# One neighbour step for both base tiles, float32r matmuls behind 512-wide ones, and a single ring of PSUM banks in a fused attention and MLP kernel

## The chip, the cores and the metric

The kernel runs on one core of one Trainium2 chip. The time is device microseconds (us) of one execution, and the metric is the median over runs. A run more than 1.5% above the fastest of the same kernel is called slow here and is left out of ratios. TensorE is called PE, VectorE DVE, ScalarE ACT, as in the profile.

## The reference

```python
def _attn_ref(x, inducing):            # x [4, 12480, 128], inducing [32, 128]
    ...
    def mab(q, kv):
        s = scale * (q @ kv.transpose(0, 2, 1))
        s = s - s.max(-1, keepdims=True)
        a = np.exp(s)
        a /= a.sum(-1, keepdims=True) + 1e-09
        return a @ kv
    h = mab(I, x)                      # 32 rows per batch
    return mab(x, h)

def _moe_ref(x, w_in, w_out):          # w_in [128, 2048], w_out [2048, 128]
    h = x @ w_in
    relu6 = np.clip(h + 3.0, 0.0, 6.0)
    return (h * relu6 / 6.0) @ w_out
```

The second attention mixes only 32 rows h of its batch. Where the hidden values stay inside the clip's range, the MLP of such a mix is a linear term in the 32 weights plus a quadratic one in the pairs of weights. So the kernel first reads a batch to find its h and makes coefficients from it; then each token needs only exponentials, and matmuls against the coefficients.

## The kernel before

A batch has 25 chunks: 24 of four tiles of 128 tokens, and a short one. Four chunks are a group; the short chunk is a group by itself. For each chunk, two matmuls `bp` and their exponentials give two **base tiles** of pair features. The column set `W[k]` holds h(m) + h(m+2+2k+4i), so base 0 has the pairs at distances 2, 6, 10, ... and base 1 those at 4, 8, 12, ... The odd distances come from a **neighbour step**: base 0 times exp(h(m+1) - h(m)) gives distances 1, 5, ..., and times exp(h(m-1) - h(m)) gives 3, 7, ...

```python
# coefficients of a batch
Wd = coef.tile([P, 2, M], BF16, name="Wd")            # two neighbour steps
nc.vector.tensor_sub(Wd[:, 0], HT2[:, 1 : M + 1], HT[:, 0])           # shortened
nc.vector.tensor_sub(Wd[:, 1], HT2[:, M - 1 : 2 * M - 1], HT[:, 0])   # shortened
...
def b_pack(b, g, k):            # one group's neighbour factors, k = 0, 1
    pp = psF.tile([P, 512], FP32, name="pp", tag="fb")
    for j in range(J):          # four tiles of 32 columns, side by side
        nc.tensor.matmul(pp[32 * j : 32 * j + 32, :w], lhsT=st["Wd"][:, k], rhs=..., tile_position=(0, 32 * j))
    t = dpk.tile([P, 512], BF16, name=f"dk{k}")
    nc.scalar.activation(t[: 32 * J, :w], pp[: 32 * J, :w], ACT.Exp, scale=scale)
def b_spread(b, c):             # each row to four partitions, by DMA
    for k in range(2):
        d = dp.tile([P, 512], BF16, name=f"d{k}")
        nc.sync.dma_start(d[:, :w], st[("dk", g, k)][...].unsqueeze(1).to_broadcast([32, 4, w]))
def b_prod(b, c):
    for k in range(2):
        d = st.pop(("d", c, k))
        nc.vector.tensor_mul(t[:, :w], T0[:, :w], d[:, :w])
...
def b_f(b, g):                  # sums of the exponentials e
    nc.tensor.matmul(sp[:, : J * p], lhsT=blk[:, :], rhs=e[:, : J * p])          # float32r
    # nf = -e * sp
def b_r(b, g):                  # 1 / sum, a whole group at once
    for j in range(J):
        nc.tensor.matmul(rp[:p, j * SL : (j + 1) * SL], lhsT=nf[:, j * p : (j + 1) * p], rhs=one4[:, :])  # float32r
    nc.vector.reciprocal(r_all[...], rp[:p, : J * SL])
def b_lin(b, c):                # linear term, float32r, 512 columns
    nc.tensor.matmul(op[:p, :], lhsT=nf[...], rhs=BD, start=True, stop=False)
def b_quad(b, c, s, op):        # quadratic term of one of four token tiles
    for k in range(4):
        nc.tensor.matmul(op[:p, s * C : (s + 1) * C], lhsT=T[k][:, s * p : (s + 1) * p], rhs=Cq[:, k, :])
```

While batch b gives out its results, batch b+1 is read (`xb`, `pt`, `xT`, `s`, `a`, `hnd`) and its coefficients are made: G (`gp`) and its hardswish `hs`, `L`, `BD`; `dpm` and its squares `sq`; their sums `cp`, then `Cq`. These pieces are "units", emitted between the parts of a chunk:

```python
for t in range(-LEAD - 3, total):           # one chunk; b_evac, b_spread, b_prod cut
    b_base(fb_, fc, 0)                      # bp for chunk t + 2
    bg(0.25)                                # units due by here
    op = b_lin(bo, co); b_quad(bo, co, 0, op)
    bg(0.5)
    b_quad(bo, co, 1, op)
    for fn in ahead.get(t, []): fn()        # b_pack | b_e | b_f | b_r, each in its own chunk of the group
    bg(0.75)
    b_quad(bo, co, 2, op)
    b_base(fb_, fc, 1)
    bg(1.0)
    b_quad(bo, co, 3, op)
```

PSUM has three banks in a pool `psF` (bp, pp, ep, sp, rp), two in `psX` (pt, s, dpm), two for the output and one (`psH`) for hnd, gp, lp and cp.

## Time and profile before

I cut the run at the starts of the linear products (`op<-BD,nf`) of chunks 0, 25, 50 and 75 and of the last chunk. What lies ahead of the first is the start-up; the tail is the last evacuation and the checks at the end.

| before | us |
|---|---|
| time, median of 4 runs (range; the 363.68 is a slow run) | 356.44 (354.2 to 363.68) |
| start-up | 54.00 |
| batches 0, 1, 2 (with background) | 82.62, 79.93, 79.28 |
| last batch (no background) | 46.28 |
| tail | 10.70 |
| span of the profiled run (a run of its own, 354.64) | 352.80 |

The last batch is the clean place to price an instruction, because nothing but chunks runs there. The background batches are where most of the time is. The profile's own lines stand in the prediction.

### The profile page before, as it was taken

To read this page: it belongs to the slowest core of one execution; us is meant where nothing else is said; L and a number is where in the kernel's file an instruction comes from. 1 tells how busy PE (TensorE), PEld (TensorE's weight loads), DVE (VectorE), ACT (ScalarE), POOL (GpSimd) and SP (SyncE) were. 2 spreads that over 40 slices of the span, in tenths; PEclk is the share of its full clock that TensorE was granted. 3 is DMA by queue.
4 is the path that set the end of the run, shared out by engine and by line. 5 is a ranking of instruction groups with operands and counts; after the bars stand their busy time and mean duration, and the time that the engine had idled before them with its cause. 6 is when DMAs were issued, how large, how long until landed. Compare 5 with 4: busy or idle time off the path is not lost. (4 is left out here: it accounts for less than half of the span.)

```text
span 352.8 us, 10094 instructions
## 1 busy us (share of the span) xinstructions
PE 321.2 (91%) x4001; PEld 238.6 (68%) x4026; DVE 245.5 (70%) x592; ACT 239.3 (68%) x440; POOL 17.6 (5%) x37
## 2 busy tenths in 40 slices
PE   0968989999969999999999999999999999999990
PEld 0855567787646676887667676887667776676670
DVE  4765777787587556877696556877696656777781
ACT  2433589877546988888556988888556885767740
POOL 3032000101100000010100000010000000000000
PEclk9999899999999999999999999999999999999996
DMA  7699744697994665778996576687673566789963
GB/s 268 226 349 361 271 92 91 163 333 242 354 357 156 157 178 190 204 256 217 342 403 237 136 206 194 180 258 239 144 208 132 140 207 199 224 254 252 256 211 130
DMA packets 38536, 79.54 MB, mean 225 GB/s; under 512 B 5168, under 2 KB 31824, under 8 KB 32208
## 3 DMA queue, kind: packets, MB, share of 16 engines
q1 hardware_dynamic: 32560, 51.15, 47.8%
q0 software_dynamic: 5920, 27.66, 25.2%
q8 instruction: 33, 0.54, 0.6%
q14 instruction: 23, 0.19, 0.2%
HBM read 27.67 MB, written 25.56 MB: 151 GB/s over the span
## 5 line engine op out<-in xcount | busy, mean ns | idle before, releaser
L594 PE MATMUL op<-Cq,T 128*128 128x128 bf16 (+1 forms) x1600 | 147.5, 220 | 0.5
L558 ACT ACTIVATE T<-bp 128x512 bf16<-128x512 f32 (+1 forms) x200 | 112.4, 593 | 42.6 <-PE bp L552 30.6
L594 PEld LDWEIGHTS <-T 128*128 128x128 bf16 (+1 forms) x1600 | 98.0, 98 | 42.4 <-issue 26.4
L610 DVE TENSOR_TENSOR os<-op,r_all 128x512 f32<-128x512 f32 (+1 forms) x100 | 68.7, 687 | 47.2 <-PE op L594 46.4
L569 DVE TENSOR_TENSOR T<-T,d 128x512 bf16<-128x512 bf16 (+1 forms) x200 | 74.1, 409 | 7.2 <-DMA d<-dk 6.9
L552 PE MATMUL bp<-xT,W 128*128 128x512 bf16 (+1 forms) x186 | 69.4, 374 | 0.8 <-DVE d_all L328 0.8
L206 ACT CAST xb<-xr 128x1024 bf16<-128x1024 f32 (+1 forms) x49 | 46.8, 963 | 9.6 <-DMA xr<-in_x_dram 9.6
L578 PE MATMUL op<-BD,nf 128*128 128x512 f32 (+1 forms) x100 | 52.3, 523 | 0.0
L216 DVE COPY xT<-pt 128x1024 bf16<-128x1024 bf16 (+1 forms) x56 | 34.4, 618 | 11.8 <-PE pt L215 11.5
L237 PE MATMUL hnd<-xr,a 128*32 128x128 f32 (+1 forms) x400 | 38.0, 237 | 3.2 <-ACT a L229 3.2
L427 ACT ACTIVATE sq<-dpm 128x512 bf16<-128x512 f32 x60 | 35.3, 603 | 7.0 <-PE dpm L416 5.2
L529 ACT ACTIVATE dk<-pp 128x512 bf16<-128x512 f32 (+1 forms) x56 | 28.2, 554 | 13.3 <-PE pp L522 12.7
L215 PE MATMUL pt<-ident_b,xb 128*128 128x128 bf16 (+1 forms) x400 | 32.7, 225 | 4.7 <-DVE xb L206 4.1
L237 PEld LDWEIGHTS hnd<-xr,a 128*32 128x32 f32 (+1 forms) x400 | 27.5, 111 | 9.7 <-ACT a L229 5.2
L215 PEld LDWEIGHTS <-xb 128*128 128x128 bf16 (+1 forms) x400 | 25.7, 101 | 10.5 <-DVE xb L206 4.2
L111 POOL DMA_DIRECT2D xr<-in_x_dram x28 | 15.1, 539 | 219.2 <-ACT xb L206 127.9
L436 PE MATMUL cp<-w6n,sq 128*128 128x128 bf16 x256 | 24.3, 219 | 1.6 <-DVE BD L409 0.9
L229 ACT ACTIVATE a<-s 128x512 fp32r<-128x512 f32 (+1 forms) x28 | 15.5, 553 | 15.0 <-PE s L223 15.0
L436 PEld LDWEIGHTS <-sq 128*128 128x128 bf16 x256 | 18.6, 98 | 9.2 <-DVE BD L409 1.4
L416 PE MATMUL dpm<-dH,w_in_b 128*128 128x512 bf16 x54 | 20.8, 389 | 2.7 <-DVE dH L350 2.6
L487 DVE CUSTOM_DVE_ANT_0 nf<-e,sp 128x512 fp32r<-128x512 f32 (+1 forms) x28 | 17.2, 613 | 4.7 <-PE sp L485 4.2
L552 PEld LDWEIGHTS <-W 128*128 128x128 bf16 x200 | 19.5, 98 | 0.6
(98 smaller groups left out, 270.3 us busy)
## 6 DMA issues: line engine op xcount, KB each, us to landing
xr<-in_x_dram POOLq DMA_DIRECT2D x24, 1024.0 KB, 7.5
d<-dk SPq DMA_DIRECT2D x192, 128.0 KB, 3.9
out_dram<-os SPq DMA_DIRECT2D x24, 1024.0 KB, 4.1
w_in_r<-in_moe_w_in_dram POOLq DMA_DIRECT2D x1, 1024.0 KB, 5.8
w_out_r<-in_moe_w_out_dram POOLq DMA_DIRECT2D x1, 1024.0 KB, 9.6
xr<-in_x_dram POOLq DMA_DIRECT2D x4, 96.0 KB, 5.9
d<-dk SPq DMA_DIRECT2D x8, 48.0 KB, 3.7
out_dram<-os SPq DMA_DIRECT2D x4, 96.0 KB, 3.2
```

The lines of the kernel that those rows point to most:

```text
L206: eng(xb[:p, lo:hi, :], xs[(b, g)][:p, lo:hi, :].bitcast(FP32))
L215: nc.tensor.transpose(pt[:, (i - lo) * p : (i - lo + 1) * p], xb[:p, i, :], ident_b[:p, :p])
L216: nc.vector.tensor_copy(st["xT"][:, t0 + lo * p : t0 + hi * p], pt[:, : (hi - lo) * p])
L237: nc.tensor.matmul(st["hnd"][:M, :C], lhsT=a1[:p, i * M : (i + 1) * M], rhs=xs[(b, g)][:p, i, :], start=(g == 0 and i == 0), stop=(g == NG ...
L427: nc.scalar.activation(sq[:, :], dpm[:, :], ACT.Square)
L436: nc.tensor.matmul(st["cp"][:, k * C : (k + 1) * C], lhsT=sq[:, k * P : (k + 1) * P], rhs=w6n[:, jc, :], start=(jc == 0 and k == 0), stop= ...
L552: nc.tensor.matmul(bp[:, :w], lhsT=st["W"][:, k].rearrange("p m i -> p (m i)"), rhs=st["xT"][:, c0 : c0 + w],)
L558: nc.scalar.activation(t[:, :w], bp[:, :w], ACT.Exp, scale=scale)
L569: nc.vector.tensor_mul(t[:, :w], T0[:, :w], d[:, :w])
L578: nc.tensor.matmul(op[:p, :], lhsT=st[("nf", g)][:, j * p : (j + 1) * p], rhs=st["BD"][:, :], start=True, stop=False, skip_group_check=True,)
L594: nc.tensor.matmul(op[:p, s * C : (s + 1) * C], lhsT=T[k][:, s * p : (s + 1) * p], rhs=st["Cq"][:, k, :], start=False, stop=(s == SL - 1 a ...
L610: nc.vector.tensor_mul(ot[:p, j * SL : (j + 1) * SL, :], op[:p, :].rearrange("p (s c) -> p s c", c=C), r_all[:p, b, c, :].unsqueeze(2).to_ ...
```

## The change

The intent: shorten PE's stream, since PE sets the time.

1. One neighbour step d = exp(h(m+1) - h(m)) for **both** base tiles. Base 0 times d has distances 1, 5, ...; base 1 times the same d pairs m+1 with m+4+4i, distances 3, 7, ... Half of pp, of its exponentials, and of the transfers go away, and one multiply of 1024 columns replaces two of 512. pp and ep are emitted together.
2. rp is taken one chunk at a time, behind a `bp`.
3. sp stands behind the other `bp`.
4. So does the linear product, in every chunk (behind sp where there is one).
5. For batches 1 to 3, the G matmuls stand singly behind the 512-wide dpm.
6. For batches 1 to 3, the coefficient sums cp follow after all 16 squares.
7. psF and psX become one ring of five banks, which cp of batches 1 to 3 also draws on.
8. Smaller things go with it: the four products of a tile are taken in the order 0, 3, 1, 2 (base tiles first), and `hs` becomes a unit of its own.

```diff
-        psF = es.enter_context(tc.tile_pool(name="psF", bufs=3, space=PSUM))
+        psF = es.enter_context(tc.tile_pool(name="psF", bufs=5, space=PSUM))
-        psX = es.enter_context(tc.tile_pool(name="psX", bufs=2, space=PSUM))
...
-            Wd = coef.tile([P, 2, M], BF16, name="Wd")
+            Wd = coef.tile([P, M], BF16, name="Wd")
...
+                us += [lambda jb=jb: (c_sq(b, jb), c_G(b, jb, jb + 1)) for jb in range(FB)]
+                us += ls[0:1] + cs[0:4] + ls[1:3] + cs[4:8] + ls[3:] + cs[8:]
...
+            nc.tensor.matmul(rp[:p, :SL], lhsT=nf[:, j * p : (j + 1) * p], rhs=one4[:, :])
+            nc.vector.reciprocal(r_all[:p, b, c, :], rp[:p, :SL])
...
+            u = tp.tile([P, 2, 512], BF16, name="TD")
+            nc.vector.tensor_mul(u[:, :, :w], t[:, :, :w], d[:, :w].unsqueeze(1).to_broadcast([P, 2, w]))
+            st[("T", c)] = [t[:, 0], u[:, 0], u[:, 1], t[:, 1]]
...
-            for k in range(4):
+            for k in (0, 3, 1, 2):
...
+                ahead.setdefault(t - LEAD - 3, []).append(lambda b=b, g=g: (b_pack(b, g), b_e(b, g)))
+                sums[t - LEAD - 1] = (b, g)
...
             if feat:
                 b_base(fb_, fc, 0)
-            bg(0.25)
+            if t in sums:
+                b_f(*sums[t])
             if t >= 0:
                 op = b_lin(bo, co)
                 b_quad(bo, co, 0, op)
-            bg(0.5)
+            bg(0.33)
...
-            bg(0.75)
+            bg(0.67)
+            if feat:
+                b_base(fb_, fc, 1)
+            if 0 <= t + 1 < total:
+                b_r(*divmod(t + 1, NCK))
             if t >= 0:
                 b_quad(bo, co, 2, op)
-            if feat:
-                b_base(fb_, fc, 1)
```

More of the change, by code (lines that the diff above doesn't have):

```diff
@@ L27 @@
 XBUF = 4
-CLAG = 6
 LEAD = 2
@@ L92 @@
         cst = es.enter_context(tc.tile_pool(name="cst", bufs=1))
-        sqp = es.enter_context(tc.tile_pool(name="sqp", bufs=8))
+        sqp = es.enter_context(tc.tile_pool(name="sqp", bufs=FB))
         coef = es.enter_context(tc.tile_pool(name="coef", bufs=2))
         PSUM = bass.MemoryType.PSUM
-        psF = es.enter_context(tc.tile_pool(name="psF", bufs=3, space=PSUM))
+        psF = es.enter_context(tc.tile_pool(name="psF", bufs=5, space=PSUM))
         psO = es.enter_context(tc.tile_pool(name="psO", bufs=2, space=PSUM))
-        psX = es.enter_context(tc.tile_pool(name="psX", bufs=2, space=PSUM))
         psH = es.enter_context(tc.tile_pool(name="psH", bufs=1, space=PSUM))
@@ L186, in side_bank @@
                     return psO.tile(shape, dtype, name=name, tag="op")
-            return psX.tile(shape, dtype, name=name, tag="pt")
+            return psF.tile(shape, dtype, name=name, tag="fb")
         S = {}
@@ L349, in c_HT, with c_G @@
             nc.vector.tensor_sub(dH[:, 0], shifted(HT, 0, 1, 0), shifted(HT, 2, 0, 4))
-            nc.vector.tensor_sub(dH[:, 1], shifted(HT, M - 1, 1, 0), shifted(HT, 2, 2, 4))
+            nc.vector.tensor_sub(dH[:, 1], shifted(HT, 1, -1, 0), shifted(HT, 4, 0, 4))
             W = coef.tile([P, 2, M, 4], BF16, name="W")
             nc.vector.tensor_add(W[:, :], shifted(HT, 0, 0, 0), shifted(HT, 2, 2, 4))
-            Wd = coef.tile([P, 2, M], BF16, name="Wd")
-            nc.vector.tensor_sub(Wd[:, 0], HT[:, :, :].rearrange("p a m -> p (a m)")[:, 1 : M + 1], HT[:, 0])
-            nc.vector.tensor_sub(Wd[:, 1], HT[:, :, :].rearrange("p a m -> p (a m)")[:, M - 1 : 2 * M - 1], HT[:, 0])
+            Wd = coef.tile([P, M], BF16, name="Wd")
+            nc.vector.tensor_sub(Wd[:, :], HT[:, :, :].rearrange("p a m -> p (a m)")[:, 1 : M + 1], HT[:, 0])
             st["W"], st["Wd"] = W, Wd
-        def c_G(b, h):
+        def c_G(b, lo, hi):
             st = S[b]
-            if h == 0:
+            if lo == 0:
                 st["gp"] = psH.tile([P, 512], FP32, name="gp", tag="hnd")
             gp = st["gp"]
-            for jb in range(8 * h, 8 * h + 8):
+            for jb in range(lo, hi):
                 nc.tensor.matmul(
@@ L369, in c_G, with c_hs @@
                 )
-            if h == 0:
-                return
+        def c_hs(b):
+            st = S[b]
+            gp = st["gp"]
             r6 = cst.tile([P, 512], FP32, name="r6")
@@ L413, in c_sq, with c_C @@
             st = S[b]
-            if jb < FB:
-                dpm = side_bank(b, [P, 512], FP32, "dpm")
-                nc.tensor.matmul(
-                    dpm[:, :],
-                    lhsT=w_in_b[:, jb * P : (jb + 1) * P],
-                    rhs=st["dH"][:, :, :, :, :].rearrange("p q k m i -> p (q k m i)"),
-                )
-                sq = sqp.tile([P, 512], BF16, name="sq")
-                if b == 0 and jb % 4 == 3:
-                    d32 = cst.tile([P, 512], FP32, name="d32")
-                    nc.vector.tensor_copy(d32[:, :], dpm[:, :])
-                    nc.vector.tensor_mul(sq[:, :], d32[:, :], dpm[:, :])
-                else:
-                    nc.scalar.activation(sq[:, :], dpm[:, :], ACT.Square)
-                st[("sq", jb)] = sq
-            jc = jb - CLAG
-            if jc < 0:
-                return
+            dpm = side_bank(b, [P, 512], FP32, "dpm")
+            nc.tensor.matmul(
+                dpm[:, :],
+                lhsT=w_in_b[:, jb * P : (jb + 1) * P],
+                rhs=st["dH"][:, :, :, :, :].rearrange("p q k m i -> p (q k m i)"),
+            )
+            sq = sqp.tile([P, 512], BF16, name="sq")
+            if b == 0 and jb % 4 == 3:
+                d32 = cst.tile([P, 512], FP32, name="d32")
+                nc.vector.tensor_copy(d32[:, :], dpm[:, :])
+                nc.vector.tensor_mul(sq[:, :], d32[:, :], dpm[:, :])
+            else:
+                nc.scalar.activation(sq[:, :], dpm[:, :], ACT.Square)
+            st[("sq", jb)] = sq
+        def c_C(b, jc):
+            st = S[b]
             if jc == 0:
-                st["cp"] = psH.tile([P, 512], FP32, name="cp", tag="hnd")
+                st["cp"] = (psH if b == 0 else psF).tile([P, 512], FP32, name="cp", tag="hnd" if b == 0 else "fb")
             sq = st.pop(("sq", jc))
@@ L454, in c_units @@
         def c_units(b):
-            sq = [lambda jb=jb: c_sq(b, jb) for jb in range(FB + CLAG)]
             gap = [lambda: None]
             us = [lambda: c_sum(b)] + gap + [lambda: c_den(b)] + gap + [lambda: c_HT(b)] + gap
-            us += sq[0:1] + [lambda: c_G(b, 0), lambda: c_G(b, 1)] + sq[1:3]
-            us += [lambda: c_L(b, 0), lambda: c_L(b, 1)] + sq[3:5] + [lambda: c_BD(b)]
-            us += sq[5:] + [lambda: c_tail(b)]
-            return us
+            cs = [lambda jc=jc: c_C(b, jc) for jc in range(FB)]
+            ls = [lambda: c_hs(b), lambda: c_L(b, 0), lambda: c_L(b, 1), lambda: c_BD(b)]
+            if b == 0:
+                sq = [lambda jb=jb: c_sq(b, jb) for jb in range(FB)]
+                us += sq[0:1] + [lambda: c_G(b, 0, 8), lambda: (c_G(b, 8, FB), c_hs(b))] + sq[1:3]
+                us += ls[1:3] + sq[3:5] + ls[3:] + sq[5:7]
+                for jb in range(7, FB):
+                    us += [cs[jb - 7], sq[jb]]
+                us += cs[FB - 7 :]
+            else:
+                us += [lambda jb=jb: (c_sq(b, jb), c_G(b, jb, jb + 1)) for jb in range(FB)]
+                us += ls[0:1] + cs[0:4] + ls[1:3] + cs[4:8] + ls[3:] + cs[8:]
+            return us + [lambda: c_tail(b)]
         def b_e(b, g):
@@ L497, in b_f, with b_r, b_pack @@
             st[("nf", g)] = nf
-        def b_r(b, g):
+        def b_r(b, c):
+            g, j = chunks[c]
             t0, p, n = groups[g]
-            st = S[b]
-            J = n // SL
-            nf = st[("nf", g)]
+            nf = S[b][("nf", g)]
             rp = psF.tile([P, 512], FP32, name="rp", tag="fb")
-            for j in range(J):
-                nc.tensor.matmul(
-                    rp[:p, j * SL : (j + 1) * SL], lhsT=nf[:, j * p : (j + 1) * p], rhs=one4[:, :]
-                )
-            c0 = first_chunk[g]
-            nc.vector.reciprocal(
-                r_all[:p, b, c0 : c0 + J, :].rearrange("p j s -> p (j s)"), rp[:p, : J * SL]
-            )
-        def b_pack(b, g, k):
+            nc.tensor.matmul(rp[:p, :SL], lhsT=nf[:, j * p : (j + 1) * p], rhs=one4[:, :])
+            nc.vector.reciprocal(r_all[:p, b, c, :], rp[:p, :SL])
+        def b_pack(b, g):
             t0, p, n = groups[g]
@@ L523, in b_pack @@
                     pp[32 * j : 32 * j + 32, :w],
-                    lhsT=st["Wd"][:, k],
+                    lhsT=st["Wd"][:, :],
                     rhs=st["xT"][:, t0 + j * w : t0 + (j + 1) * w],
@@ L527, in b_pack @@
                 )
-            t = dpk.tile([P, 512], BF16, name=f"dk{k}")
+            t = dpk.tile([P, 512], BF16, name="dk")
             nc.scalar.activation(t[: 32 * J, :w], pp[: 32 * J, :w], ACT.Exp, scale=scale)
-            st[("dk", g, k)] = t
+            st[("dk", g)] = t
         def b_spread(b, c):
@@ L536, in b_spread @@
             w = SL * groups[g][1]
-            for k in range(2):
-                d = dp.tile([P, 512], BF16, name=f"d{k}")
-                nc.sync.dma_start(
-                    d[:, :w],
-                    st[("dk", g, k)][32 * j : 32 * j + 32, :w].unsqueeze(1).to_broadcast([32, 4, w]),
-                )
-                st[("d", c, k)] = d
+            d = dp.tile([P, 512], BF16, name="d")
+            nc.sync.dma_start(
+                d[:, :w],
+                st[("dk", g)][32 * j : 32 * j + 32, :w].unsqueeze(1).to_broadcast([32, 4, w]),
+            )
+            st[("d", c)] = d
         def b_base(b, c, k):
@@ L556, in b_base @@
             )
-            t = tp.tile([P, 512], BF16, name=f"T{3 * k}")
-            nc.scalar.activation(t[:, :w], bp[:, :w], ACT.Exp, scale=scale)
-            st[("x", c, k)] = t
+            if k == 0:
+                st[("x", c)] = tp.tile([P, 2, 512], BF16, name="TF")
+            nc.scalar.activation(st[("x", c)][:, k, :w], bp[:, :w], ACT.Exp, scale=scale)
         def b_prod(b, c):
@@ L563, in b_prod @@
             w = SL * groups[chunks[c][0]][1]
-            T0, T3 = (st.pop(("x", c, k)) for k in range(2))
-            T = [T0]
-            for k in range(2):
-                d = st.pop(("d", c, k))
-                t = tp.tile([P, 512], BF16, name=f"T{1 + k}")
-                nc.vector.tensor_mul(t[:, :w], T0[:, :w], d[:, :w])
-                T.append(t)
-            st[("T", c)] = T + [T3]
+            t = st.pop(("x", c))
+            d = st.pop(("d", c))
+            u = tp.tile([P, 2, 512], BF16, name="TD")
+            nc.vector.tensor_mul(u[:, :, :w], t[:, :, :w], d[:, :w].unsqueeze(1).to_broadcast([P, 2, w]))
+            st[("T", c)] = [t[:, 0], u[:, 0], u[:, 1], t[:, 1]]
         def b_lin(b, c):
@@ L598, in b_quad @@
                     start=False,
-                    stop=(s == SL - 1 and k == 3),
+                    stop=(s == SL - 1 and k == 2),
                     skip_group_check=True,
@@ L646 @@
         total = B * NCK
-        ahead = {}
+        ahead, sums = {}, {}
         for b in range(B):
@@ L650 @@
                 t = b * NCK + first_chunk[g]
-                ahead.setdefault(t - LEAD - 3, []).append(lambda b=b, g=g: (b_pack(b, g, 0), b_pack(b, g, 1)))
-                ahead.setdefault(t - LEAD - 2, []).append(lambda b=b, g=g: b_e(b, g))
-                ahead.setdefault(t - LEAD - 1, []).append(lambda b=b, g=g: b_f(b, g))
-                ahead.setdefault(t - LEAD, []).append(lambda b=b, g=g: b_r(b, g))
+                ahead.setdefault(t - LEAD - 3, []).append(lambda b=b, g=g: (b_pack(b, g), b_e(b, g)))
+                sums[t - LEAD - 1] = (b, g)
         for b in range(1, B):
```

## The prediction

> **What bounds the kernel now.** I read the page first, then the busy time of each engine in chosen stretches, then the timeline of TensorE (PE) in the last batch. The kernel has a start-up of 54 us, then four batches of 25 chunks. While batches 0 to 2 give out their results, the next batch is read in and its coefficients are made ("background"); the last batch has none.
>
> ```profile
> PE 321.2 (91%) x4001; PEld 238.6 (68%) x4026; DVE 245.5 (70%) x592; ACT 239.3 (68%) x440; POOL 17.6 (5%) x37
> ...
> 0.00:54.00 54.00, 39.16 (x468) 29.03 (x472) 34.92 (x85) 25.69 (x43) 8.55 (x20) 0.97 0.83 256
> ...
> 136.63:216.55 79.92, 78.12 (x999) 58.70 (x1004) 57.48 (x136) 60.95 (x113) 3.73 (x7) 1.00 0.76 242
> 295.83:342.11 46.28, 46.28 (x539) 32.83 (x540) 36.00 (x90) 32.24 (x63) 0.00 (x0) 1.00 0.86 248
> ```
>
> The columns of a stretch are its length, then busy us of PE, weight load, VectorE (DVE), ScalarE (ACT), GpSimd. PE is busy for 78.1 of 79.9 us in batch 1 and for all of the last batch; DVE and ACT stand at 72 and 76% in batch 1. So PE's instruction stream sets the time after 54 us, and what shortens it shortens the run, until another engine comes up to it. What an instruction costs there is the distance between starts, not its printed length (lengths overlap). The stream in the last batch:
>
> ```profile
> 326.05 0.58 PE L578 MATMUL op<-BD,nf 128*128 128x512 f32 x1
> 326.48 0.62 PE L594 MATMUL op<-Cq,T 128*128 128x128 bf16 x8
> 327.03 0.62 PE L522 MATMUL pp<-xT,Wd 128*32 128x512 bf16 x8
> 327.58 0.40 PE L594 MATMUL op<-Cq,T 128*128 128x128 bf16 x4
> ...
> 329.25 0.40 PE L471 MATMUL ep<-xT,HTb 128*32 128x512 bf16 x4
> ...
> 330.26 0.38 PE L552 MATMUL bp<-xT,W 128*128 128x512 bf16 x1
> 330.29 0.58 PE L578 MATMUL op<-BD,nf 128*128 128x512 f32 x1
> 330.71 0.62 PE L594 MATMUL op<-Cq,T 128*128 128x128 bf16 x8
> 331.14 0.47 PE L485 MATMUL sp<-e,blk 128*128 128x512 f32 x1
> ...
> 332.16 0.58 PE L578 MATMUL op<-BD,nf 128*128 128x512 f32 x1
> 332.58 0.62 PE L594 MATMUL op<-Cq,T 128*128 128x128 bf16 x8
> 333.01 0.59 PE L506 MATMUL rp<-one,nf 128*128 128x4 f32 x4
> 333.46 0.40 PE L594 MATMUL op<-Cq,T 128*128 128x128 bf16 x4
> ```
>
> Four chunks make a group. L578 starts at 326.05, 328.28, 330.29, 332.16 and 334.16: intervals of 2.23, 2.01, 1.87 and 2.01, 8.1 us a group. Each chunk has 16 products of L594 at 0.056 (0.90), two bp at 0.216 (0.43) and one L578: 1.58. What is above that are the group's extras, one a chunk: pp 0.65, ep 0.43, sp 0.29, rp 0.43. They can be checked singly: rp, 333.46 minus 332.58 is 0.88, less eight L594 (0.45), is 0.43, or 0.106 for each of four. Where background runs, L578 often stands behind a 128-wide matmul, and the matmuls of G (64 in all) run in rows:
>
> ```profile
> 139.78 0.61 PE L215 MATMUL pt<-ident_b,xb 128*128 128x128 bf16 x8
> 140.20 0.48 PE L578 MATMUL op<-BD,nf 128*128 128x512 f32 x1
> 140.52 0.40 PE L594 MATMUL op<-Cq,T 128*128 128x128 bf16 x4
> ...
> 184.50 1.15 PE L365 MATMUL gp<-HTr,w_in_r 128*128 128x32 f32 x8
> 185.50 0.48 PE L578 MATMUL op<-BD,nf 128*128 128x512 f32 x1
> ```
>
> Behind pt: 140.52 minus 139.78, less eight times 0.056, leaves 0.29 for L578. Behind bp (330.26 to 330.71, less 0.216) it is 0.235. The float32r matmul is 0.055 cheaper behind a 512-wide one. G runs at 0.112 each within a row.
>
> [...]L578 is entered 0.03 us after bp starts, and costs least there. [...]eight pp cost only 0.22 more than four ep. [...]The bf16 multiplies before run so (starts 0.333 apart for 512 columns, 0.165 for 192, so 1.9 a ns).
>
> **The change, part by part (PE).**
> 1. One neighbour step: four pp instead of eight, emitted right before ep. Four tiles alone cost 0.43 (as ep), eight cost 0.65. pp plus ep becomes one run of eight tiles: 0.65 in place of 0.65 + 0.43. Gain 0.43 x 24 full groups, plus an estimated 0.3 for each of the four short groups: 11.5 us.
> 2. rp is taken one chunk at a time, each behind bp. Its load hides under bp's 0.216; left are the 0.02 that L578 pays there too, and 4 columns, about 0.03 (the 32-column s matmuls start 0.025 apart). Estimate 0.05 for 0.106, 96 times: 5.4 us.
> 3. sp behind bp: 0.24 for 0.29, 24 times: 1.2 us. L578 then follows sp and I keep 0.24 for it.
> 4. L578 now always follows bp or sp, apart from the last chunks. By the starts, 46 of 100 did before (25 of them in the last batch). 54 x 0.055: 3.0 us.
> 5. G one by one behind the 512-wide dpm for batches 1 to 3: 48 x (0.112 - 0.05): 3.0 us.
>
> Sum 24.1 us. About 1.2 of it falls in the start-up, where PE waits anyway: 23 us. Moving the sums (cp) behind the squares changes no count: 256 at 0.056 as before.
>
> Other engines: ACT loses 28 exponentials (28 x 0.48 between starts = 13 us, off the path). On DVE two multiplies of 512 columns (2 x 0.333) become one of 1024 (0.333 + 512/1.9 ns = 0.60), while 28 reciprocals become 100 at 0.17 to 0.19: about +1 us a batch. Neighbour transfers fall from 200 to 100, some 12 MB less. DVE waited 6.9 us for them, but PE had none of that in the last batch: worth under 1 us.
>
> What comes back: a background batch goes to about 73 us with 58 of ACT and 58.5 of DVE, 79 and 80% in place of 76 and 72. Counting ACT's work by emitted order, the 16 squares now fall in five chunks: ten T, 16 squares, dk and e are 28 x 0.48 = 13.4 us against 13.4 of PE. There PE and ACT run neck and neck. I allow 1.3 us more waiting per background batch, 4 in all. Net 19: span 352.8 to 333.8; the profiled run took 1.8 more than its span: 335.6. With the scatter of the median, 336.
>
> **Rivals.**
> - *Squares and banks become the bound.* The five-bank ring serves dpm, bp, rp and background together, and cp holds one bank to the end. If PE stalls behind ACT in the square stage and behind DVE in the read-in stage, 3 us more a batch: 344. For it: ACT equals PE there. Against: three plus two separate banks cost only 1.8 us of PE idle a batch. Chance 15%.
> - *Short float32r matmuls do not get cheap.* If rp and G keep their 0.11 behind a wide one, 8.4 us are lost: 344. Against: the first G of the row behind bp, by 185.50 minus 184.48, less 0.216 and seven times 0.112, cost some 0.02 to 0.05. Chance 12%.
> - [...]DVE then needs 2.1 us a chunk against PE's 1.8 in the last batch, and 71 us in a background batch: about 355. [...]Chance 4%.
>
> **Range and chances.** Two rivals end near 344. On the good side, no added waiting gives 331, a faster start-up 330. Range 329 to 344. Faster by over 2% means under 349.4, which only the third rival or two of them together miss: 0.93; within 2% 0.05; slower 0.02.
>
> **What will show it.** Right: a group of the last batch takes 7.4 us (4 x 1.58, 0.65, 0.24, 4 x 0.05) for 8.1, that window 43 us; bp to the product after rp is 0.27; a background batch takes 73 to 75; the one multiply lasts 0.68 us. Wrong: the bp-rp-product distance near 0.32 (rival two); idle PE before dpm, bp or pt with ACT or DVE as releaser (rival one); a multiply of 1.1 us (rival three). If the chunk is short but the batches stay near 80 us, my allowance for waits was the failing step.

## The result

The changed kernel takes 333.03 us (median of 4 runs, 332.65 to 333.91) against 356.44. The ratio of fast runs is 0.9348, 95% interval 0.9289 to 0.9407. Ratios here and below are taken over fast runs of the same rounds, so not quite the ratio of the medians quoted. The result is correct, as is that of every run below.

| us | start-up | batch 0 | batch 1 | batch 2 | last batch | tail | span | a group of the last batch |
|---|---|---|---|---|---|---|---|---|
| before | 54.00 | 82.62 | 79.93 | 79.28 | 46.28 | 10.70 | 352.80 | 8.11 |
| after | 54.30 | 74.85 | 74.00 | 73.99 | 42.27 | 12.12 | 331.53 | 7.33 |
| difference | +0.3 | -7.8 | -5.9 | -5.3 | -4.0 | +1.4 | -21.3 | -0.78 |

First, the first part of the page after the change:

```profile
PE 300.7 (91%) x3926; PEld 236.3 (71%) x3926; DVE 242.1 (73%) x560; ACT 228.2 (69%) x412; POOL 17.7 (5%) x37
```

PE's share is the 91% it had: it lost 20.5 us of work and the span lost 21.3. The stretches after (length; busy us of PE, weight load, DVE, ACT, GpSimd; clock; DMA share; GB/s), cut at the linear products:

```profile
54.30:129.15 74.85, 72.88 (x982) 57.76 (x979) 56.43 (x128) 58.49 (x108) 3.75 (x7) 1.00 0.63 207
129.15:203.15 74.00, 72.53 (x980) 57.64 (x979) 56.30 (x128) 57.57 (x106) 3.75 (x7) 1.00 0.67 218
...
277.13:319.40 42.27, 42.27 (x522) 32.78 (x522) 36.33 (x86) 31.08 (x57) 0.00 (x0) 1.00 0.64 204
```

PE is busy in all of the last batch, as before, and idle for 1.5 us of batch 1 (1.8 before). ACT and DVE have 78 and 76% of batch 1. The DMA share of the last batch fell from 0.86 to 0.64, since half of the neighbour transfers went. PE's timeline of the last batch shows what each moved instruction costs:

```profile
293.39 0.38 PE L551 MATMUL bp<-xT,W 128*128 128x512 bf16 x1
293.42 0.58 PE L492 MATMUL sp<-e,blk 128*128 128x512 f32 x1
293.84 0.39 PE L575 MATMUL op<-BD,nf 128*128 128x512 f32 x1
294.06 0.28 PE L591 MATMUL op<-Cq,TF 128*128 128x128 bf16 x2
...
294.52 0.38 PE L551 MATMUL bp<-xT,W 128*128 128x512 bf16 x1
294.55 0.35 PE L511 MATMUL rp<-one,nf 128*128 128x4 f32 x1
294.77 0.28 PE L591 MATMUL op<-Cq,TF 128*128 128x128 bf16 x2
...
297.64 0.28 PE L591 MATMUL op<-Cq,TD 128*128 128x128 bf16 x2
297.85 0.40 PE L522 MATMUL pp<-xT,Wd 128*32 128x512 bf16 x4
298.07 0.39 PE L478 MATMUL ep<-xT,HTb 128*32 128x512 bf16 x4
298.39 0.39 PE L551 MATMUL bp<-xT,W 128*128 128x512 bf16 x1
```

Read the starts. From bp (294.52) to the product behind rp (294.77) is 0.25, and bp alone is 0.216, so **rp costs 0.03** (0.032 at the trace's full resolution), where it cost 0.106. From bp (293.39) to the product behind the linear one (294.06) is 0.67: less 0.216, two float32r matmuls of 512 columns cost 0.23 each. The joint run of pp and ep, from 297.64 plus two products (0.11) to 298.39, is 0.64, where two runs were 0.65 + 0.43. Together they give the group: 0.30 (four rp at 0.074 less) + 0.44 + 0.06 (sp) is 0.80, against 0.78 measured.

The multiplies, from the costliest groups (count, busy us, mean ns, idle ahead), before and then after:

```profile
L569 DVE TENSOR_TENSOR T<-T,d 128x512 bf16<-128x512 bf16 (+1 forms) x200 | 74.1, 409 | 7.2 <-DMA d<-dk 6.9
```

```profile
L567 DVE TENSOR_TENSOR TD<-TF,d 128x1024 bf16<-128x1024 bf16 (+1 forms) x100 | 66.8, 668 | 3.9 <-ACT TF L558 2.1
```

One multiply of 1024 columns takes 668 ns, less than two of 409: the broadcast operand did not halve the rate, which was the third rival (by an estimate, 1024 columns at half of the 1.9 results a ns measured before would take 1.1 us). The idle time of DVE that d ended fell from 6.9 us to 1.5 (the second entry of the changed kernel's line in the answer by groups).

### The profile page after: what moved, and what is told of

Same layout as the page of the kernel before. It is cut to its first block, busy times and chain, and to the rows that moved or that the text cites. A ratio compares the mean times of both kernels' runs of the same rounds, so it can differ in the third digit from the quotient of the medians.

```text
span 331.5 us, 9598 instructions
## 1 busy us (share of the span) xinstructions
PE 300.7 (91%) x3926; PEld 236.3 (71%) x3926; DVE 242.1 (73%) x560; ACT 228.2 (69%) x412; POOL 17.7 (5%) x37
## 4 chain that ended last, share of the span: by engine, by line
PE 80%; DVE 8%; ACT 5%; issue 2%; DMA 2%; POOL 1%; POOLq 0%; DVEq 0%
PE op L591 27%; PE bp L551 12%; PE hnd L235 7%; PE op L575 6%; PE pt L213 6%; PE dpm L414 4%; PE cp L434 4%; PE s L221 3%; PE pp L522 2%; DVE xT L214 2%; DMA xr<-in_x_dram 2%; PE sp L492 2%; PE lp L388 1%; PE ep L478 1%; ACT xb L204 1%
## 5 line engine op out<-in xcount | busy, mean ns | idle before, releaser
L558 ACT ACTIVATE TF<-bp 128x512 bf16<-128x512 f32 (+1 forms) x200 | 118.7, 601 | 35.0 <-PE rp L511 18.2
L591 PE MATMUL op<-Cq,TF 128*128 128x128 bf16 (+1 forms) x800 | 109.7, 223 | 0.2 <-DVE Cq L447 0.2
L591 PE MATMUL op<-Cq,TD 128*128 128x128 bf16 (+1 forms) x800 | 106.5, 219 | 0.0
L551 PE MATMUL bp<-xT,W 128*128 128x512 bf16 (+1 forms) x200 | 75.1, 376 | 0.0
L591 PEld LDWEIGHTS <-TF 128*128 128x128 bf16 (+1 forms) x800 | 50.4, 98 | 34.0 <-issue 25.5
L567 DVE TENSOR_TENSOR TD<-TF,d 128x1024 bf16<-128x1024 bf16 (+1 forms) x100 | 66.8, 668 | 3.9 <-ACT TF L558 2.1
L591 PEld LDWEIGHTS <-TD 128*128 128x128 bf16 (+1 forms) x800 | 61.5, 98 | 0.2 <-issue 0.2
L575 PE MATMUL op<-BD,nf 128*128 128x512 f32 (+1 forms) x100 | 52.9, 529 | 0.0
L512 DVE RECIPROCAL r_all<-rp 128x4 f32<-128x4 f32 (+1 forms) x100 | 17.7, 177 | 23.0 <-PE rp L511 22.8
L511 PE MATMUL rp<-one,nf 128*128 128x4 f32 (+1 forms) x100 | 34.5, 345 | 0.0
L414 PE MATMUL dpm<-dH,w_in_b 128*128 128x512 bf16 x64 | 24.1, 389 | 0.9 <-ACT w_in_b L637 0.6
## 6 DMA issues: line engine op xcount, KB each, us to landing
w_out_r<-in_moe_w_out_dram POOLq DMA_DIRECT2D x1, 1024.0 KB, 10.2
```

What stands on the lines that cost most here:

```text
L414: nc.tensor.matmul(dpm[:, :], lhsT=w_in_b[:, jb * P : (jb + 1) * P], rhs=st["dH"][:, :, :, :, :].rearrange("p q k m i -> p (q k m i)"),)
L551: nc.tensor.matmul(bp[:, :w], lhsT=st["W"][:, k].rearrange("p m i -> p (m i)"), rhs=st["xT"][:, c0 : c0 + w],)
L558: nc.scalar.activation(st[("x", c)][:, k, :w], bp[:, :w], ACT.Exp, scale=scale)
L567: nc.vector.tensor_mul(u[:, :, :w], t[:, :, :w], d[:, :w].unsqueeze(1).to_broadcast([P, 2, w]))
L575: nc.tensor.matmul(op[:p, :], lhsT=st[("nf", g)][:, j * p : (j + 1) * p], rhs=st["BD"][:, :], start=True, stop=False, skip_group_check=True,)
```

## The experiments

Each experiment alters the changed kernel in one place, but for e5 and e7: to make room, both give TD three buffers instead of four, and e5 gives `e` two instead of three. Their stages come from the profiled run, one execution each. Stages that an edit does not touch repeat closely (the last batch is 42.27 in the changed kernel, e6, e8 and e9b). The start-up varies from 52.9 to 56.3 us and the tail from 10.7 to 12.6 between kernels that hardly differ there, so the arguments below use the stages between. The start-up goes with the clock that the traces show as granted to PE: there it falls from 1.00 to 0.50 for one stretch of 3.4 us (start-ups of 52.9 to 54.0; before the change at 38.8 us), for two (54.2 to 55.2; in the changed kernel at 24.6 and 41.7 us), or for three, or one and another of 10.2 us (55.6 to 56.3). A run called slow counts in the median and range but not in the ratio (e5 had one). The ratio is to the kernel before in the same rounds; the changed kernel's own is 0.9348 and was measured apart, on its own rounds.

| us | batch 0 | batch 1 | batch 2 | last batch | group | median (range), 4 or 5 runs | ratio [95%] |
|---|---|---|---|---|---|---|---|
| changed kernel | 74.85 | 74.00 | 73.99 | 42.27 | 7.33 | 333.03 (332.65-333.91) | 0.9348 [0.9289, 0.9407] |
| e1_rp_rows | 75.69 | 75.17 | 75.18 | 43.88 | 7.60 | 337.79 (336.48-338.42) | 0.9508 [0.9465, 0.9552] |
| e2_rp_behind_products | 75.94 | 75.12 | 74.90 | 43.75 | 7.57 | 337.04 (335.18-338.91) | 0.9499 [0.9443, 0.9554] |
| e3_lin_behind_products | 76.20 | 75.37 | 75.36 | 43.80 | 7.57 | 339.27 (336.65-339.97) | 0.9519 [0.9454, 0.9585] |
| e4_ep_apart | 74.91 | 74.05 | 74.06 | 43.86 | 7.56 | 336.03 (333.93-336.66) | 0.9459 [0.9420, 0.9499] |
| e8_G_rows | 76.14 | 75.31 | 75.31 | 42.27 | 7.33 | 337.75 (335.01-338.23) | 0.9448 [0.9354, 0.9542] |
| e5_two_packs | 77.00 | 77.17 | 75.67 | 44.33 | 7.56 | 346.01 (342.41-349.91) | 0.9740 [0.9621, 0.9858] |
| e6_two_multiplies | 74.78 | 73.95 | 73.94 | 42.27 | 7.33 | 333.28 (332.14-333.83) | 0.9328 [0.9262, 0.9395] |
| e7_neighbour_twice | 75.74 | 73.94 | 73.92 | 46.24 | 7.34 | 338.50 (334.25-341.95) | none: two of four slow |
| e9_sums_between | 78.99 | 81.24 | 76.61 | 42.43 | 7.33 | 349.26 (343.83-353.14) | none: two of four slow |
| e9b_sums_between | 75.15 | 74.29 | 74.30 | 42.27 | 7.33 | 333.36 (333.16-333.65) | 0.9324 [0.9260, 0.9388] |
| e10_split_banks | 75.81 | 75.56 | 75.58 | 46.56 | 8.13 | 341.63 (340.12-342.45) | 0.9566 [0.9496, 0.9637] |
| e11_even_fill | 74.42 | 73.32 | 73.33 | 42.42 | 7.35 | 331.84 (331.37-332.23) | 0.9287 [0.9221, 0.9352] |

Against the totals expected, e1, e2 and e4 came out 2 to 3 us shorter, e3, e8 and e11 1 to 2 longer, and e5 8 or more longer.

### e1: rp in rows of four again

```diff
-            if 0 <= t + 1 < total:
-                b_r(*divmod(t + 1, NCK))          # one chunk, behind bp
+   # b_r(b, g) does the four of a group into one bank, one reciprocal; called once a group, as before the change
```

> Undoes one part: the four rp of a group in one row behind the products, as before the change. Theory (the stream of TensorE sets the time[...]): in the trace of the changed kernel an rp behind bp costs 0.032 us (bp to the next product 0.248, less 0.216), in a row 0.106; 96 x 0.074 = 7.1 us more, so about 340 us, a group of the last batch 7.3 + 4 x 0.074 = 7.6 us, a background batch 1.8 us longer. Rival (the waits on VectorE and ScalarE now set the time, so that TensorE has room): under 2 us more.

PE's timeline in the last batch:

```profile
291.88 0.59 PE L512 MATMUL rp<-one,nf 128*128 128x4 f32 x4
292.33 0.39 PE L557 MATMUL bp<-xT,W 128*128 128x512 bf16 x1
```

Four in a row take 0.45 again. The group is 7.60, 0.27 more than 7.33, close to 4 x 0.074 = 0.30. In the background batches the row costs 0.8 to 1.2 us, less than the 1.8 of the sum by counts; what takes up the rest is not shown.

### e2: rp one by one, but behind a 128-wide product

```diff
-            if 0 <= t + 1 < total:
-                b_r(*divmod(t + 1, NCK))
             if t >= 0:
                 b_quad(bo, co, 2, op)
+            if 0 <= t + 1 < total:
+                b_r(*divmod(t + 1, NCK))
```

> One rp a chunk as in the changed kernel, but four products later, so behind a 128-wide matmul and not behind bp. Theory (the place behind the wide matmul is what makes it cheap): each costs about 0.106 again, 7.1 us more, about 340 us. Rival (being alone is what makes it cheap, wherever it stands): under 1 us more, about 333.5 us. A lone rp here costs the start distance from the product before it to the product after it less 0.056: 0.10 by the theory, 0.03 by the rival.

```profile
289.70 0.28 PE L591 MATMUL op<-Cq,TD 128*128 128x128 bf16 x2
289.79 0.25 PE L511 MATMUL rp<-one,nf 128*128 128x4 f32 x1
289.90 0.28 PE L591 MATMUL op<-Cq,TF 128*128 128x128 bf16 x2
```

From 289.70 to 289.90 is 0.20; less two products (0.11), the same rp costs 0.09. So being single is not what makes rp cheap: the **512-wide matmul ahead of it** is. The group is 7.57; of the 0.074 that the change took off each rp, 0.06 depends on the place.

### e3: linear product and sp behind a 128-wide product

```diff
-            if feat:
-                b_base(fb_, fc, 0)
             if t in sums:
                 b_f(*sums[t])
             if t >= 0:
                 op = b_lin(bo, co)
                 b_quad(bo, co, 0, op)
+            if feat:
+                b_base(fb_, fc, 0)
```

> The first bp of a chunk moved behind the first four products, so that sp and the BD product stand behind 128-wide matmuls. Theory: 28 sp at 0.055 more and the 71 BD products that now stand behind bp at 0.055 more (those behind sp stay at 0.23): 5.4 us more, about 338.5 us. Rival (order does not matter, only counts do): 0 to 1 us more.

The group is 7.57, so 0.06 for each of its four chunks: the same 0.055 that the lines before the change had shown. It costs 1.4 us in each background batch.

### e4: ep in a run of its own

```diff
-                ahead.setdefault(t - LEAD - 3, []).append(lambda b=b, g=g: (b_pack(b, g), b_e(b, g)))
+                ahead.setdefault(t - LEAD - 3, []).append(lambda b=b, g=g: b_pack(b, g))
+                ahead.setdefault(t - LEAD - 2, []).append(lambda b=b, g=g: b_e(b, g))
```

> ep emitted one chunk after pp, as before the change; four pp and four ep each as a run of its own. Theory: a run of four column tiles costs 0.43 alone, the joint run of eight 0.64, so 0.21 more in each of 24 full groups, some 0.2 in four short ones: 5.9 us more, about 339 us; a group of the last batch 7.5 us. Rival (what counts is only the number of tiles): 0 to 1 us more.

In the last batch the group is 7.56 and the batch 1.6 us longer, as reckoned. In the background batches it costs 0.06. The reason is found by summing the distances between PE's starts over batch 1 for each pair of neighbouring instructions. Each run of four costs the same as in the last batch, so that price was paid. But ep now stands in the hole in which PE waited for `xT` before `s` (0.9 us of waits there in the changed kernel, 0.2 in e4), and the pairs s-s and op-dpm became 0.6 us shorter. So the joint run was worth 0.23 us a group where PE had no such hole, and 0.06 us in a whole batch where it had one. The profiled run is the fastest of the five (333.93; the others took 335.6 to 336.7), so whether the background batches cost nothing in those too is not known.

### e8: G in rows of eight

```diff
-                us += [lambda jb=jb: (c_sq(b, jb), c_G(b, jb, jb + 1)) for jb in range(FB)]
+                us += [lambda: (c_sq(b, 0), c_G(b, 0, 8)), lambda: (c_sq(b, 1), c_G(b, 8, FB))]
+                us += [lambda jb=jb: c_sq(b, jb) for jb in range(2, FB)]
```

> The 16 matmuls of G for batches 1 to 3 in two rows of eight, each row behind the first and second wide dpm, instead of one behind each dpm. Theory: in a row 0.112, behind dpm 0.032 (0.248 less 0.216): 14 x 0.08 = 1.1 us more in each background batch if TensorE sets the time there, 3.4 us in all, 336.4 us; the last batch the same. Rival (in the square stage ScalarE sets the time, so TensorE has room): under 0.3 us a batch.

It costs 1.3 us in each background batch and nothing in the last. By the sum over pairs of starts in batch 1, dpm and G account for 1.1 of it, the expected 14 x 0.080 (the first G of each row still stands behind a dpm); the other 0.2 lies elsewhere. That part is confirmed at its size.

### e5: two packs, two transfers, two multiplies

```diff
-   b_pack(b, g), b_e(b, g)
+   b_pack(b, g, 0), b_pack(b, g, 1), b_e(b, g)     # same Wd both times: only the work is put back
-   d = dp.tile([P, 512], BF16, name="d")           # one transfer, one multiply of 1024
+   for k in range(2): ...                          # d0 and d1, two transfers, two multiplies of 512
```

> The second neighbour step put back whole: eight pp instead of four (still in one run with ep), two exponentials, two transfers a chunk, two multiplies of 512. The second is a copy of the first, so results stay right; buffers were made room for by small cuts elsewhere. Theory: four more column tiles cost 0.22 on TensorE, so a group of the last batch goes from 7.33 to 7.55 and the last batch from 42.3 to 43.5; background batches, which the runs so far showed to take up part of such a cost in waits, 0.3 to 1.3 more each; in all 2 to 5 us, 335 to 338 us. Rival (ScalarE, VectorE or the transfers were what the single step relieved): background batches 2 us or more longer each, 340 us or above.

The group is 7.56, so the second pack costs PE 0.22, as theory had it. The rest of the theory missed: the last batch is 2.1 longer and not 1.2 (0.8 of it in one chunk, where PE waits 0.3 for a TD that stood behind ACT's `e`), the whole run 346.01 and not 335 to 338. The background batches cost more too: 2.2, 3.2 and 1.7. In batch 1 the sum over pairs of starts gives 1.4 for the second pp, and 1.4 more for one wait of PE before `dps`, the sum that ends the read-in. DVE's timeline just before it, then PE's (the bracket is the idle time ahead and its releaser):

```profile
171.25 0.43 DVE L571 TENSOR_TENSOR TD<-TF,d 128x512 bf16<-128x512 bf16 x1 [1.46 <-DMA d<-dk]
171.59 1.01 DVE L316 TENSOR_REDUCE dred<-dacc 128x32 f32<-128x512 f32 x1
```

```profile
172.74 0.20 PE L327 MATMUL dps<-ones,dred 128*32 128x2 f32 x2 [1.75 <-DVE r_all L514]
```

DVE waited 1.46 us for this d. `dred`, which has nothing to do with d, comes later in DVE's program and started only behind it (171.59), and PE waited 1.75 us for `dred` (the profile names the reciprocal right behind it). So here a late neighbour transfer reached PE over DVE's queue and cost it 1.4 us.

### e6 and e7: two multiplies; two multiplies and two transfers

```diff
 # e6
-            nc.vector.tensor_mul(u[:, :, :w], t[:, :, :w], d[:, :w].unsqueeze(1).to_broadcast([P, 2, w]))
+            for k in range(2):
+                nc.vector.tensor_mul(u[:, k, :w], t[:, k, :w], d[:, :w])
 # e7: as e6, and the second multiply reads d2, a second transfer of the same d
```

> The one multiply of 1024 columns done as two of 512 with the same neighbour step; nothing else changed. Theory (VectorE is off the path): 0.07 us more VectorE a chunk, hidden: within 0.3 us a stage of the changed kernel (74.0 a background batch, 42.3 the last). Rival (VectorE is now the bound, so that part of what two packs cost was its work): 100 x 0.07 = 7 us more, 1.7 us a batch.

> The same with each neighbour step also transferred twice (200 transfers as before the change, the second multiply reads the second copy); TensorE and ScalarE have no more work. It parts the three costs inside two packs, which came out 9 us or more slower with 1.7 to 3.2 us more a background batch against 0.3 to 1.3 expected. Theory (transfers were hidden, as predicted): as the two multiplies alone, within 1 us. Rival (fewer transfers are part of the gain, through late neighbour steps when they meet the 1 MB loads): 1 us or more longer in a background batch, with VectorE waiting for d for over 3 us, and an irregular spread of the times.

e6 is within 0.1 us of the changed kernel in each of the four batches: DVE's work is off the path. e7 has the same DVE work and twice the transfers (and three TD buffers, but no wait for one is in its records). Its times scatter from 334.25 to 341.95 (two of four called slow), where e6's and e9b's on the same chip lie between 332.1 and 333.8. In the profiled run, a fast one of 337.16, the last batch takes 46.24. Waits there (us in total, times, longest):

```profile
DVE TD L575 <- DMA d<-dk: 4.7, 4, 2.9
...
PE op L600 <- DVE TD L575: 1.8, 1, 1.8
```

The changed kernel has 0.3 us of the first and none of the second there. The lost 4.0 us follow from one place: chunk 20, where the two TD of a chunk wait for their d, costs 2.2. The other 1.7 is a slower clock. From 1.6 us after that wait, the clock granted to PE is 0.50 for 3.4 us, and the products start 0.11 apart instead of 0.056 (length; busy us of PE, weight load, DVE, ACT, GpSimd; clock; DMA share; GB/s):

```profile
317.19:320.60 3.41, 3.41 (x24) 2.64 (x23) 2.11 (x8) 1.52 (x4) 0.00 (x0) 0.50 0.97 351
```

That the wait caused the fall is not shown: the 1.75 us of e5 above was followed by none. Of the background batches only batch 0 is longer than in e6 (by 1.0, before `dps`); batches 1 and 2 are as short, so the rival, which forecast 1 us or more in a background batch, holds in one of three. So at the shorter chunk the old number of transfers is not always hidden; it costs 1 to 4 us in the two fast runs (334.25 and 337.16 against a mean of 333.1 for e6), and differs from run to run.

### e9 and e9b: the sums between the squares again

```diff
 # e9: from the seventh square on, each square and one sum are one unit (78 units become 68)
+                for jb in range(6, FB):
+                    us += [lambda jb=jb: (sq[jb](), cs[jb - 6]())]
 # e9b: the same order, but each its own unit (78 units, as in the changed kernel)
+                for jb in range(7, FB):
+                    us += [cs[jb - 7], sq[jb]]
```

> For batches 1 to 3 the coefficient sums between the squares again (six behind, as before the change), G still behind dpm. Theory (as predicted: the move changes no count and is worth little): background batches within 0.7 us of the changed kernel's 74.0. Rival one (sums behind the squares keep a bank and wait out of the square stage, and the move is a good part of the gain): 1.5 us or more longer each. Rival two (with nothing between them the squares make TensorE wait for ScalarE): 0.7 us or more shorter each.

> The sums between the squares again for batches 1 to 3, now as units of their own, so that the background has as many units as in the changed kernel and the read-in of x keeps its pace. The earlier run of this (10 to 18 us slower) joined them to the squares, which slowed the read-in: at the same chunk of every batch it waited 1.6 to 2.3 us more. Theory (the order of sums and squares itself is worth little): background batches within 0.7 us of 74.0. Rival (sums behind the squares are a good part of the gain): 1.5 us or more longer.

e9 lost 2.6 to 7.2 us in each background batch, which no theory had. Two places grew. One is chunk 7 of each batch (+1.5, +1.5, +2.3), in the read-in. The other is chunk 16 of batches 0 and 1 (+2.2, +4.5), among the squares: PE waits 2.4 and 3.7 us there for a TD whose d is late, and after the second of these waits the granted clock is 0.5 for 3.4 us. The waits in batch 1 of e9 (window 134 to 213 us):

```profile
DVE TD L570 <- DMA d<-dk: 5.7, 2, 4.8
...
ACT xb L204 <- DMA xr<-in_x_dram: 3.0, 1, 3.0
```

Units are spread evenly by their number. Fewer units in the coefficient stage make the read-in be spread over more chunks: in batch 1 its transposes end in chunk 11 instead of 9, and the last load of x is issued 41.7 us after the batch's start instead of 36.9. Three d issued beside it take 10 to 13 us to land (median of the run 4.2). My edit had changed the pace as well as the order. e9b keeps the pace: it costs 0.3 us in each background batch, and neither place grows. So moving the sums is worth 0.3 us a batch, and e9's loss goes with its pace; that joining squares and sums has no part of its own in it was not tested.

### e10: three and two banks again

```diff
-        psF = es.enter_context(tc.tile_pool(name="psF", bufs=5, space=PSUM))
+        psF = es.enter_context(tc.tile_pool(name="psF", bufs=3, space=PSUM))
+        psX = es.enter_context(tc.tile_pool(name="psX", bufs=2, space=PSUM))
# background tiles, and cp for b > 0, come from psX
```

> The five banks of the one ring split as before into three and two (background and the coefficient sums on the two). Theory: in the last batch nothing changes (no background; 42.3 us); in background batches a group of three banks for bp, rp, sp, pp and ep with one more use a chunk (rp) waits more than the 74.0 us: 1 to 3 us more each, 336 to 342 us. Rival (banks never were what TensorE waited for): within 0.5 us a batch.

I had expected the last batch to stay as it was, since it has no background. It takes 46.56, more than before the change (46.28). PE's timeline there:

```profile
295.00 0.38 PE L552 MATMUL bp<-xT,W 128*128 128x512 bf16 x1 [0.19 <-ACT TF L559]
...
298.16 0.39 PE L552 MATMUL bp<-xT,W 128*128 128x512 bf16 x1
298.72 0.27 PE L512 MATMUL rp<-one,nf 128*128 128x4 f32 x1 [0.16 <-ACT dk L530]
```

From this bp to rp is 0.56, where it is 0.03 in the changed kernel. With two bp, one rp and the group's pp, ep and sp now all drawing on three banks, PE waits until ACT has read an older one (its records of the last batch have 1.0 us at bp behind ACT's TF and 0.7 at rp behind dk). The sum over pairs of starts gives, for the last batch, bp-rp +2.5, op-bp +1.9, bp-sp +0.3, and -0.4 at rp-op: the 4.3 us. So the ring is not tidying: **with three banks for these users the new order loses all that it gained in the last batch**, and most of the loss stands at rp, which now takes a bank in every chunk. (Four banks, or three with rp in rows, were not tried.)

### e11: units emitted when due, not one ahead

```diff
-            while queue and done_units[0] < share:
+            while queue and done_units[0] + 1 <= share + 1.0e-6:
```

> A try for a faster version: a background unit is emitted only when its share is full (rounding down where the changed kernel rounds up), so the first chunk of a batch gets 16 transposes and not 24. In the changed kernel that chunk takes 5.06 us (3.58 before the change), with TensorE waiting for xT copies. Theory: 1 us or more shorter in a background batch, 73 us, 330 us in all. Rival (the wait only moves to the next chunks): 74.0 as now.

The changed kernel emits a whole group's transposes and its `s` in the first chunk of a batch, before DVE can have copied `xT`. PE's timeline at the start of batch 1, first the changed kernel's:

```profile
129.81 1.06 PE L213 MATMUL pt<-ident_b,xb 128*128 128x128 bf16 x16
...
131.80 0.36 PE L221 MATMUL s<-I_T,xT 128*128 128x32 bf16 x8 [0.72 <-DVE xT L214]
```

Then that of e11:

```profile
130.36 0.61 PE L213 MATMUL pt<-ident_b,xb 128*128 128x128 bf16 x8
...
132.58 0.36 PE L221 MATMUL s<-I_T,xT 128*128 128x32 bf16 x8 [0.23 <-DVE xT L214]
```

The wait of 0.72 us is down to 0.23: eight transposes are followed by products, and DVE copies meanwhile. The first chunk of batch 1 takes 3.88 us in place of 5.06. The batch gains 0.7, not the 1 or more expected: by the sum over pairs of starts, the waits before `s` and `dps` shrank by 1.3, and one of 0.5 before `htp` came up. Its four runs (331.4 to 332.2) lie below the eight of e6 and e9b on the same chip (332.1 to 333.8), but for an overlap of 0.1 us. It is the fastest version, by some 0.4%; the gap to the changed kernel itself was not measured in common rounds.

## Why the prediction was right

The prediction was 336.0 in a range of 329 to 344; the result is 333.03. Its signs came too: the group takes 7.33 us (7.4 forecast), the last batch 42.3 (43), the background batches 74.0 to 74.9 (73 to 75), bp to the product after rp 0.25 (0.27), the one multiply 0.668 (0.68). Its steps:

- **PE sets the time.** Right: the span shrank by what PE's stream did, and extra DVE work (e6) changed nothing.
- **Part 1, pp and ep.** Right in size: 0.64 measured for 0.65. e4 adds that in a background batch the joint emission by itself is worth nothing in this order of units, since ep filled a hole that the changed kernel has at the start of the batch; the second pp (e5) is worth its 0.22 a group everywhere.
- **Part 2, rp, and part 5, G.** Right that they get cheap behind a wide matmul (e1, e2, e8), and the size too careful: both cost 0.032 and not 0.05. The trace after the change shows the weight load of rp, 0.19 us, starting with bp at 294.52 and so inside bp's 0.216. With the measured size, rp is 96 x 0.074 = 7.1 instead of 5.4. Of the 48 G, one a batch stood behind a bp before and was cheap already, so G is 45 x 0.080 = 3.6 instead of 3.0. These are the mis-sized terms that made the prediction some microseconds long.
- **Parts 3 and 4, sp and the linear product.** Right: 0.23 each for 0.24, and e3 gives the 0.06 back. A count was off: of the 46 linear products behind a bp before, 22 and not 25 are in the last batch, and two of the last chunks have no bp ahead in either kernel, so 52 gain and not 54.
- **The waits that come back.** I allowed 4 us. With the measured sizes, the parts sum to 11.8 + 7.1 + 1.4 + 2.9 + 3.6 = 26.8, or 25.6 without the 1.2 of the start-up. The four batches gained 23.0. So 2.6 were lost again. By the records of waits, PE waits 1.3 us in batch 1 (0.9 of it for `xT` before `s`, which the kernel before did not have) against 1.3 before; so the records don't show where the 2.6 went, and I leave it open. The experiments point to two parts: in batch 1, rows of rp cost 1.2 and not the 1.8 of their count (e1), separate runs 0.06 and not 1.3 (e4). The allowance's stated cause, ACT keeping PE back in the squares, is not what shows: no wait of PE for a square's bank is in those records. One rp near the end of the squares starts 0.31 behind its bp in each background batch, where 0.03 is usual, and 0.2 is lost; what it waits for is not shown. So that the allowance came near was luck.
- **Neighbour transfers, "worth under 1 us".** Wrong. Put back by themselves (e7) they cost 1 to 4 us in fast runs, and in e5 a late d cost PE 1.4 us in one batch. What failed was the inference from the kernel before, where PE had no such wait at its longer chunk. It did no harm to the sum, because the change removes the transfers together with the time in which they hid.
- **Load of DVE.** Wrong in sign: in batch 1 it fell from 57.5 to 56.3 us, where about 1 us more was forecast (its own terms give 1.6). DVE is off the path (e6), so nothing came of it.
- **The ring of banks.** The prediction had it only as a danger. e10 shows it to be a condition: with three and two banks the last batch takes 46.56. That is worth 4.3 us in the last batch and 1.0 to 1.6 in each other, in no term of the sum; the sum silently assumed that a bank is always free.
- **Rivals.** The float32r matmuls did get cheap behind a wide one (0.032, not 0.11); the one multiply took 0.668 us and so kept its rate; the squares did not become the bound. The third rival's multiply can be estimated from the starts measured before the change: at half of 1.9 results a ns, and with the 0.06 us that 512 columns (0.333) and 192 (0.165) leave fixed, it would take 1.14 us. That the rate would be kept was my estimate; no run before the change showed it. The start-up (+0.3) and the tail (+1.4) took back 1.7 us, which is within what they vary by between nearly equal kernels.

So the total owes something to luck: parts that gained 2.6 more than forecast, waits 1.4 smaller than allowed, and ends that took back 1.7 make the span 2.3 us shorter than the 333.8 forecast.

## What to carry to other kernels

Price an instruction of a busy engine by the distance between starts in a stretch where nothing else runs, and ask what stands ahead of it: the same 4-column float32r matmul cost 0.03 or 0.09 us depending on that alone (e2). Cutting a row of small matmuls into single ones paid here with five banks in one ring and not with three (last batch 42.27 us and 46.56, e10), so count the banks that the new order takes at once before you count its gain. An experiment on the order of work must keep the pace of everything that is spread by number (2.6 to 7.2 us a background batch in e9, 0.3 in e9b), and a transfer that was hidden behind a long chunk must be checked again when the chunk gets shorter (1 to 4 us in the fast runs of e7). Where a stretch is longer than its waits, look at the granted clock before you look for another wait (in e7, 0.50 for 3.4 us cost 1.7).
